# Opening loads of a fused attention and MLP kernel: another queue for the first v, w_in in more parts

## The chip, the cores and the metric

The kernel runs on one core of a Trainium2 chip. The metric is the device time of one execution in microseconds (us), lower is better. The time before is 259.38 us, the median of three runs (259.32 to 259.7).

## The reference

Eight batches of eight heads with 576 rows of 64 columns go through a linear attention: k and v are multiplied into a 64x64 matrix per head, q is multiplied by that, and each row is divided by its root mean square and scaled by g_norm. The result, 4608 rows of 512 columns, goes through a two-layer network with 2048 hidden columns and a sigmoid gate.

```
kv = np.einsum('bhsd,bhse->bhde', k, v)
out = np.einsum('bhsd,bhde->bhse', q, kv)
rms = np.sqrt(np.mean(out * out, axis=-1, keepdims=True) + 1e-06)
x = (out / rms * g_norm)          # then heads beside each other: 4608 x 512
h = x @ w_in                      # 512 x 2048
g = h * (1.0 / (1.0 + np.exp(-1.702 * h)))
return g @ w_out                  # 2048 x 512
```

Inputs and output are float32 in HBM; the kernel multiplies in float16.

## The kernel before

The rows are worked in nine tiles of 512 (`NT = B + 1`): tile t holds the first 512 rows of batch t, and tile 8 the remaining 64 rows of all batches. Tile t's two matrix products run while the attention of a later batch is put between them. Tiles 1 to 8 do both products by a scheme of seven products on halves (lines 589 and 709), with sums formed by VectorE. The order of work is written out by hand, engine by engine; each engine runs its own instructions in that order.

The change concerns the opening. The attention of batch 0 is computed in four head pairs (c = 0 to 3). For each pair TensorE transposes q (`a0.q(c)`, line 439, which needs the identity `ident`), multiplies k by v (`a0.kv(c)`, line 262), and VectorE masks the product with `ones2` (line 429). Then TensorE multiplies q by it (`a0.out(c)`, line 307), sums squares with `ones2` (`a0.ss(c)`, line 384), and VectorE scales (`a0.apply(c)`, line 394). Between these stand `busy` matmuls on zeros (line 869). Then the first layer of tile 0 follows (`Hidden.mm`, line 478), column block by column block of w_in in the order of `COLS`, and the second layer (`project_all`, line 822), in which four blocks of w_out's rows are used at a time. A block is 128 columns of w_in, or 128 rows of w_out; there are 16 of each.

Three queues start transfers. SyncE's queue loads pair 0's k, q and v as float32 into a staging tile `qf` (line 161), and ScalarE or VectorE casts them to float16 (lines 860 to 862). GpSimd's queue loads everything else and casts on the way: q, k, v of the pairs 1 to 3 (line 91), then w_in in parts (`load_w_in(f0, f1, k0, k1)`, line 180: column blocks f0 to f1, row blocks k0 to k1), then w_out (`load_w_out`, line 209) mixed with batch 1's q, k and v. Each load of GpSimd's queue waits until the eighth load before it has landed. ScalarE's queue loads g_norm.

The output of a tile is stored from `osb` by SyncE (line 852), the tiles in `HALVED` in two halves as soon as each half is complete, the others whole. There are two such buffers.

Of the kernel before, what the change touches and what calls it, by code (L numbers as in the profile page):

```python
# [8 lines left out]
F32 = mybir.dt.float32  # L9
# [3 lines left out]
P = 128  # L13
# [3 lines left out]
def kernel(  # L17
# [10 lines left out]
    nc = tc.nc  # L28

    B, H, S, D = q.shape  # L30
# [3 lines left out]
    FO = DFF // P  # L34
    KO = DM // P
# [7 lines left out]
    PE_ = 96  # L43
# [6 lines left out]
    stage = ctx.enter_context(tc.tile_pool(name="stage", bufs=4))  # L50
# [18 lines left out]
    vbuf = const.tile([P, NPAIR, 2 * NJ * D], F16)  # L69
    ident = const.tile([P, P], F16)  # L70
    ones2 = const.tile([P, P], F16)
# [15 lines left out]
    def early_src(n, b, c0, c1):  # L87
        return srcs[n][b, 2 * c0 : 2 * c1].rearrange("h (p j) d -> p h (j d)", j=NJ)

    def early_load(n, b, c0, c1):  # L90
        nc.gpsimd.dma_start(  # L91
            out=raw[n][0:PE_, c0:c1, :].rearrange("p c (l x) -> p (c l) x", l=2),
            in_=early_src(n, b, c0, c1),
        )
# [57 lines left out]
            )  # L152

    first = {}
    for n in "kqv":
        if n != "q":
            rows = stage.tile([P, 6, 2 * P], F32, name="qf", tag="qf", bufs=2)
            rows = rows.rearrange("p h x -> p (h x)")[0:PE_]
        first[n] = rows[:, (n == "q") * 2 * NJ * D :][:, 0 : 2 * NJ * D]
        dst, src = first[n].rearrange("p (h x) -> p h x", h=2), early_src(n, 0, 0, 1)  # L160
        nc.sync.dma_start(out=dst, in_=src)
    g_row = const.tile([1, D], F32)
    nc.scalar.dma_start(out=g_row, in_=g_norm.unsqueeze(0))
    nc.vector.memset(ident, 0.0)
    nc.vector.memset(kvb[1], 0.0)
    nc.gpsimd.affine_select(
        out=ident,
        in_=ident,
# [3 lines left out]
        pattern=[[-1, P]],  # L172
        channel_multiplier=1,
    )
    nc.gpsimd.memset(ones2, 0.0)
    nc.gpsimd.memset(ones2[0:D, 0:D], 1.0)
    nc.gpsimd.memset(ones2[D:P, D:P], 1.0)

    def load_w_in(f0, f1, k0=0, k1=KO):
        nc.gpsimd.dma_start(  # L180
            out=w_in_sb[:, k0:k1, f0 * P : f1 * P],
            in_=moe_w_in[k0 * P : k1 * P, f0 * P : f1 * P].rearrange(
                "(ko ki) f -> ki ko f", ki=P
            ),
        )

    for c in range(1, NPAIR):
        for n in "qkv":
            early_load(n, 0, c, c + 1)
# [4 lines left out]
    load_w_in(8, 10, 1, 3)  # L194
    load_w_in(0, 4, 3, KO)
    load_w_in(8, 10, 3, KO)
    load_w_in(10, 12)
    load_w_in(4, 6)
    load_w_in(6, 8)
    load_w_in(12, FO)  # L200

    nc.scalar.preload_act_table_set("abs_reciprocal_sqrt_and_small")
    nc.vector.memset(eps_t, EPS)
# [415 lines left out]
    class Seven:  # L619
# [60 lines left out]
        def place(self, name, mo, with_, i, j):  # L680
# [9 lines left out]
            if self.t == B:  # L690
# [3 lines left out]
                else:  # L694
                    store_rest(2 + mo, j * HN, (j + 1) * HN)
            elif self.t in HALVED and j == 1 - i:
                store(self.t, 2 * i, 2 * i + 2)
# [34 lines left out]
    def store_rest(mo, n0, n1):  # L732
        osb = osbs[B]
        for g in range(2):
            rows = out[(2 * mo + g) * S : (2 * mo + g + 1) * S, n0:n1]
            if 2 * mo + g < EARLY:
                p0 = SM % PE_
                rows = rows[bass.DynSlice(NJ * p0 + SM // PE_, R, step=NJ), :]
            else:
                rows = rows[SM:S, :]  # L740
            late = mo == 2 and n0 > 0
            queue = nc.gpsimd if mo == 0 or late else (nc.sync, nc.scalar)[g]
            queue.dma_start(out=rows, in_=osb[g * R : (g + 1) * R, mo, n0:n1])  # L743
# [43 lines left out]
    def layers(t, units1, units2):  # L787
# [11 lines left out]
        else:  # L799
            project_all(hid.gT, units2)  # L800
        if EARLY <= t < B and t not in HALVED:
            store(t, 0, J)
# [11 lines left out]
    def project_all(gT, units):  # L814

        os = {}

        def project(mo, fo):
            if fo == 0:
                pool, tag = (ps_h, "hT") if mo < 2 else (ps_o, "o")  # L820
                os[mo] = pool.tile([P, DM], F32, name="o", tag=tag)
            nc.tensor.matmul(  # L822
                os[mo],
                gT[:, fo, mo * P : (mo + 1) * P],
                w_out_sb[:, fo, :],
                start=(fo == 0),
                stop=(fo == FO - 1),
            )
            if fo == FO - 1:
                copy = nc.scalar.copy if mo % 2 else nc.vector.tensor_copy  # L830
                copy(osbs[0][:, mo, :], os[mo])

        steps = [(mo, 4 * i + k) for i in range(3) for mo in range(4) for k in range(4)]
        steps += [(mo, fo) for fo in (12, 13) for mo in range(4)]
        steps += [(mo, 14 + k) for mo in range(4) for k in range(2)]
        for n, (mo, fo) in enumerate(steps):
            project(mo, fo)
            for u in units.get(n, ()):
                u()
# [11 lines left out]
    def store(t, j0, j1):  # L851
        nc.sync.dma_start(
            out=out[t * S : t * S + SM, :].rearrange("(p j) m -> p j m", j=J)[:, j0:j1],
            in_=osbs[t][:, j0:j1],
        )
# [3 lines left out]

    nc.scalar.copy(qraw[0:PE_, 0, :], first["q"])  # L860
    nc.vector.tensor_copy(kraw[0:PE_, 0, :], first["k"])
    nc.vector.tensor_copy(vbuf[0:PE_, 0, :], first["v"])


    idle_ps = ps_h.tile([P, SM], F32, name="idle", tag="hT")
# [110 lines left out]
    def plan(t):  # L976
        return SECOND if t < EARLY else LATER if t < B - 1 else LAST_TWO

    HALVED = (2, 3, 4, 5)
    live = {0: a0}  # L980

    def start(b):
# [136 lines left out]
```

## Time and profile before

| what | value |
|---|---|
| median of three runs | 259.38 us |
| the profiled execution | 259.57 us |
| its span, first to last instruction | 257.8 us |
| TensorE (PE) busy | 249.9 us, 97% of the span |
| VectorE (DVE) busy | 193.8 us, 75% |
| ScalarE (ACT) busy | 177.0 us, 69% |
| GpSimd (POOL) busy | 59.6 us, 23% |
| granted TensorE clock | 0.999 |

Times in rows are us from the start of the span. In a row of a timeline stand the start, the duration, the engine, the line of the kernel, the operation and the tiles (written <- read), and in brackets how long the engine had been idle before and what ended that. PEld is TensorE's loading of weights, which runs beside its matmuls. A name followed by q (SPq, POOLq) is the queue that issues transfers. In rows of transfers stand the size of each as it is written, and the time from the start of the issue to the landing.

### The profile page before, as it was taken

The numbers are of one execution on the slowest core, as the hardware profiler recorded it, in microseconds if no ns is written. First come the engines' busy times: TensorE is split into PE (matmuls) and PEld (weight loads), VectorE is DVE, ScalarE is ACT, GpSimd is POOL, SyncE is SP. The second block draws the span as 40 slices with busy tenths as digits, with TensorE's granted clock in tenths as the row PEclk, the third lists the DMA queues.
The fourth block names the chain that finished last, engine by engine and source line by source line (L and its number), as shares of the span: only waits on it lengthen the run. The fifth ranks groups of instructions, "written<-read, shape, count | busy, mean of one in ns | idle before, by whom it ended". The sixth has DMA issues, their size and how long they took to land.

```text
span 257.8 us, 6355 instructions
## 1 busy us (share of the span) xinstructions
PE 249.9 (97%) x2596; PEld 203.6 (79%) x2596; DVE 193.8 (75%) x341; ACT 177.0 (69%) x322; POOL 59.6 (23%) x97
## 2 busy tenths in 40 slices
PE   7799999999999999999999999999999999999994
PEld 2443444788888888888888888898888888888883
DVE  1557565999958886798679867986899687857872
ACT  3468834988759894889579957995799469536800
POOL 8794245504071013301250134000000000000013
PEclk9999999999999999999999999999999999999999
DMA  7999999998999979999999799908600430012005
GB/s 175 195 168 203 204 203 200 191 160 134 194 157 200 153 90 189 184 290 112 188 184 162 84 204 144 183 4 130 210 4 0 84 163 3 0 60 106 3 19 145
DMA packets 69263, 35.33 MB, mean 137 GB/s; under 512 B 38034, under 2 KB 66834, under 8 KB 68978
## 3 DMA queue, kind: packets, MB, share of 16 engines
q0 software_dynamic: 38208, 18.31, 56.2%
q1 hardware_dynamic: 30624, 16.29, 27.2%
q8 instruction: 20, 0.33, 0.5%
q10 hardware_dynamic: 402, 0.33, 0.4%
q14 instruction: 9, 0.07, 0.1%
HBM read 36.70 MB, written 9.44 MB: 179 GB/s over the span
## 4 chain that ended last, share of the span: by engine, by line
PE 84%; DMA 11%; POOL 2%; issue 1%; DVE 0%
PE o L709 38%; PE h L589 38%; DMA w_out_sb<-in_moe_w_out_dram 7%; PE o L822 3%; DMA w_in_sb<-in_moe_w_in_dram 3%; DMA qraw<-in_q_dram 2%; POOL w_in_sb L180 2%; PE kvp L250 2%; PE outR L337 1%; PE ss L384 1%; PE kvp L262 0%; PE outT L307 0%; PE outT L311 0%; POOL vbuf L91 0%; DVE osb L689 0%
## 5 line engine op out<-in xcount | busy, mean ns | idle before, releaser
L566 ACT ACTIVATE gT<-h 128x512 f16<-128x512 f32 x96 | 52.4, 602 | 5.7 <-PE h L589 5.7
L589 PEld LDWEIGHTS <-ws 128*128 128x128 f16 x512 | 50.1, 98 | 5.9
L709 PEld LDWEIGHTS <-gS 128*128 128x128 f16 x512 | 49.1, 98 | 6.1 <-DVE gS L641 0.3
L589 PE MATMUL h<-xS,ws 128*128 128x256 f16 x384 | 52.2, 273 | 0.0
L709 PE MATMUL o<-tw,gS 128*128 128x256 f16 x384 | 45.6, 273 | 0.0
L589 PEld LDWEIGHTS <-w_in_sb 128*128 128x128 f16 x384 | 37.5, 98 | 4.7
L709 PEld LDWEIGHTS <-gT 128*128 128x128 f16 x384 | 37.6, 98 | 4.3
L709 PE MATMUL o<-w_out_sb,gT 128*128 128x256 f16 x256 | 31.4, 273 | 0.0
L589 PE MATMUL h<-xT,w_in_sb 128*128 128x256 f16 x224 | 31.1, 273 | 0.0
L603 DVE TENSOR_TENSOR h<-h,s 128x512 f32<-128x512 f32 x32 | 22.3, 698 | 4.6 <-PE h L589 3.0
L686 DVE TENSOR_TENSOR osb<-o,qf 128x512 f32<-128x512 f32 (+1 forms) x25 | 16.7, 668 | 11.3 <-PE o L709 11.3
L605 DVE TENSOR_TENSOR s<-h,s 128x512 f32<-128x512 f32 x32 | 22.1, 691 | 4.1 <-PE h L589 3.3
L743 POOL DMA_DIRECT2D out_dram<-osb x6 | 3.2, 539 | 93.2 <-DVE osb L686 93.2
L641 DVE TENSOR_TENSOR gS<-gT 128x512 f16<-128x512 f16 (+2 forms) x32 | 21.3, 684 | 0.7 <-ACT gT L566 0.6
L566 ACT ACTIVATE gT<-s 128x512 f16<-128x512 f32 x32 | 19.8, 628 | 2.8 <-DVE s L605 2.8
L589 PE MATMUL h<-xS,w_in_sb 128*128 128x256 f16 x128 | 18.9, 273 | 0.0
L535 DVE COPY s<-h 128x512 f32<-128x512 f32 x19 | 13.0, 685 | 7.7 <-PE h L589 7.6
L353 DVE TENSOR_REDUCE sum<-sq 128x8 f32<-128x512 f16 x24 | 14.9, 679 | 4.7 <-ACT sq L347 4.7
L325 ACT ACTIVATE sq<-outT 128x512 f16<-128x512 f32 (+1 forms) x16 | 7.8, 493 | 15.4 <-PE outT L307 9.9
L993 ACT ACT_TABLE_LOAD x14 | 18.0, 1283 | 0.2
L115 POOL DMA_DIRECT2D kraw<-in_k_dram x7 | 6.0, 856 | 48.6 <-PE kvp L250 32.7
L535 ACT COPY h<-h 128x512 f32<-128x512 f32 x27 | 15.4, 577 | 2.1 <-PE h L589 1.8
(105 smaller groups left out, 366.4 us busy)
## 6 DMA issues: line engine op xcount, KB each, us to landing
out_dram<-osb SPq DMA_DIRECT2D x8, 512.0 KB, 5.6
kraw<-in_k_dram POOLq DMA_DIRECT2D x5, 512.0 KB, 6.3
vbuf<-in_v_dram POOLq DMA_DIRECT2D x5, 512.0 KB, 9.8
out_dram<-osb SPq DMA_DIRECT2D x2, 1024.0 KB, 4.6
qraw<-in_q_dram POOLq DMA_DIRECT2D x3, 512.0 KB, 11.3
qbuf<-in_q_dram POOLq DMA_DIRECT2D x3, 512.0 KB, 12.5
out_dram<-osb SPq DMA_DIRECT2D x6, 192.0 KB, 6.5
w_out_sb<-in_moe_w_out_dram POOLq DMA_DIRECT2D x2, 512.0 KB, 12.7
```

The source lines that it names most:

```text
L325: nc.scalar.activation(sq[:, 0:n], t, AFT.Square)
L353: nc.vector.tensor_reduce(out=self.sum4[:, j, :], in_=self.o[j][1].rearrange("p (x d) -> p x d", d=D), op=ALU.add, axis=mybir.AxisListType.X,)
L535: (nc.vector.tensor_copy if engine == "D" else nc.scalar.copy)(to, src)
L566: nc.scalar.activation(self.gT[:, to, n * TH : (n + 1) * TH], src, AFT.Gelu_apprx_sigmoid)
L589: nc.tensor.matmul(bank[name][:, a], w, x, start=(p in (1, 5) and a == 0 and k == 0), stop=(k == KH - 1), skip_group_check=True,)
L603: nc.vector.tensor_add(bank["z"], bank["x"], self.s5)
L605: nc.vector.tensor_add(self.s5, bank["x"], self.s5)
L641: op(s[:, n, lo], a, b)
L686: nc.vector.tensor_add(o, ps, self.kept[with_][:, m])
L709: nc.tensor.matmul(o, a, w, start=(p in (1, 2, 5) and i == 0 and (mo == 0 or split)), stop=(i == HF - 1), skip_group_check=True,)
L822: nc.tensor.matmul(os[mo], gT[:, fo, mo * P : (mo + 1) * P], w_out_sb[:, fo, :], start=(fo == 0), stop=(fo == FO - 1),)
L993: u2.setdefault(i, []).append(lambda: f(*args))
```

## The change

Pair 0's v is no longer loaded by SyncE and cast by VectorE: it is GpSimd's first load, straight into `vbuf`. VectorE instead of GpSimd sets `ones2`, and GpSimd instead of VectorE clears `ident` before it writes the diagonal. The load of w_in's column blocks 10 and 11 is split by rows into two, that of blocks 12 to 15 by columns into two. Tile 6 joins the tiles that are stored in halves.

```
     first = {}
-    for n in "kqv":
-        if n != "q":
-            rows = stage.tile([P, 6, 2 * P], F32, name="qf", tag="qf", bufs=2)
-            rows = rows.rearrange("p h x -> p (h x)")[0:PE_]
+    rows = stage.tile([P, 6, 2 * P], F32, name="qf", tag="qf", bufs=2)
+    rows = rows.rearrange("p h x -> p (h x)")[0:PE_]
+    for n in "kq":
         first[n] = rows[:, (n == "q") * 2 * NJ * D :][:, 0 : 2 * NJ * D]
         dst, src = first[n].rearrange("p (h x) -> p h x", h=2), early_src(n, 0, 0, 1)
         nc.sync.dma_start(out=dst, in_=src)
...
-    nc.vector.memset(ident, 0.0)
     nc.vector.memset(kvb[1], 0.0)
+    nc.gpsimd.memset(ident, 0.0)
...
-    nc.gpsimd.memset(ones2, 0.0)
-    nc.gpsimd.memset(ones2[0:D, 0:D], 1.0)
-    nc.gpsimd.memset(ones2[D:P, D:P], 1.0)
+    nc.vector.memset(ones2, 0.0)
+    nc.vector.memset(ones2[0:D, 0:D], 1.0)
+    nc.vector.memset(ones2[D:P, D:P], 1.0)
...
+    early_load("v", 0, 0, 1)
     for c in range(1, NPAIR):
...
-    load_w_in(10, 12)
+    load_w_in(10, 12, 0, 2)
+    load_w_in(10, 12, 2, KO)
     load_w_in(4, 6)
     load_w_in(6, 8)
-    load_w_in(12, FO)
+    load_w_in(12, 14)
+    load_w_in(14, FO)
...
-    nc.vector.tensor_copy(vbuf[0:PE_, 0, :], first["v"])
...
-    HALVED = (2, 3, 4, 5)
+    HALVED = (2, 3, 4, 5, 6)
```

GpSimd's instructions at the start of the kernel, before (`qraw`, `kraw` and `vbuf` are the float16 tiles of q, k and v, `ones_98` is `ones2`; the loads of 96x2x384 are those of one head pair):

```order
L166 AFFINE_SELECT ident<-ident 128x128
L175 MEMSET ones_98 128x128
L176 MEMSET ones_98 64x64
L177 MEMSET ones_98 64x64
L91 DMA qraw<-in_q_dram 96x2x384
L91 DMA kraw<-in_k_dram 96x2x384
L91 DMA vbuf<-in_v_dram 96x2x384
```

The same place now, with the line numbers of the changed kernel:

```order
L164 MEMSET ident 128x128
L165 ISA
L165 AFFINE_SELECT ident<-ident 128x128
L91 DMA vbuf<-in_v_dram 96x2x384
L91 DMA qraw<-in_q_dram 96x2x384
L91 DMA kraw<-in_k_dram 96x2x384
L91 DMA vbuf<-in_v_dram 96x2x384
```

The memsets of the ones are gone, that of the identity is new, and one load stands ahead of the nine that were there.

Further on in GpSimd's order come the last loads of w_in and the first of w_out, before:

```order
L180 DMA w_in_sb<-in_moe_w_in_dram 128x256
L180 DMA w_in_sb<-in_moe_w_in_dram 128x4x256 x3
L180 DMA w_in_sb<-in_moe_w_in_dram 128x4x512
L209 DMA w_out_sb<-in_moe_w_out_dram 128x4x512
L91 DMA qraw<-in_q_dram 96x8x384
```

And now:

```order
L179 DMA w_in_sb<-in_moe_w_in_dram 128x256
L179 DMA w_in_sb<-in_moe_w_in_dram 128x2x256 x2
L179 DMA w_in_sb<-in_moe_w_in_dram 128x4x256 x4
L211 DMA w_out_sb<-in_moe_w_out_dram 128x4x512
L91 DMA qraw<-in_q_dram 96x8x384
```

Four loads have become six: two of two row blocks each for column blocks 10 and 11, then four of two column blocks each, where the last had four.

VectorE's first instructions, before (`kvb_88` is the tile on which the `busy` matmuls work, `qT` the transposed q, `kv_180` the product of k and v of pair 0):

```order
L164 MEMSET ident 128x64
L165 MEMSET kvb_88 128x256
L203 MEMSET eps_t 128x1
L205 MEMSET one_t 1x1
L861 COPY kraw<-qf 96x768
L862 COPY vbuf<-qf 96x768
L445 COPY qT<-q_163 128x576
L429 TENSOR_TENSOR kvb_87<-kv_180,ones_98 128x128
```

And now:

```order
L163 MEMSET kvb_88 128x256
L174 MEMSET ones_98 128x64
L175 MEMSET ones_98 64x64
L176 MEMSET ones_98 64x64
L205 MEMSET eps_t 128x1
L207 MEMSET one_t 1x1
L863 COPY kraw<-qf 96x768
L447 COPY qT<-q_163 128x576
L431 TENSOR_TENSOR kvb_87<-kv_180,ones_98 128x128
```

The cast of v between those of k and the copy of q is gone, and the three memsets of the ones stand ahead. TensorE's instructions and ScalarE's computing ones are in the same order as before.

## The prediction

> **What bounds the kernel now.** I read the page first, then the timeline of TensorE, the chain of waits, and the table by stage. The page says that TensorE is busy nearly always, apart from the opening, and that the transfers are busy all through the opening.
>
> ```profile
> span 257.8 us, 6355 instructions
> PE   7799999999999999999999999999999999999994
> DMA  7999999998999979999999799908600430012005
> ```
>
> The change touches the opening and one store near 205 us, so the question is what time the opening hands on to the rest. The table by stage (busy us of each engine with the number of its instructions, granted clock, DMA share, GB/s) has this for all that follows the opening:
>
> ```profile
> 47.00:257.80 210.80, 207.12 (x2262) 183.60 (x2260) 167.69 (x283) 150.78 (x281) 31.66 (x49) 1.00 0.76 125
> ```
>
> 207.1 of 210.8 us are TensorE's own work at full clock: whatever the opening is late or early at 47 us, the end is late or early by the same. In the opening, TensorE's timeline shows what it waits for:
>
> ```profile
> 13.34 0.38 PE L262 MATMUL kv<-vbuf,kraw 96*64 96x64 f16 x12 [0.62 <-DMA vbuf<-in_v_dram]
> 24.70 4.49 PE L478 MATMUL hT<-xT,w_in_sb 128*128 128x512 f16 x20 [0.55 <-DMA w_in_sb<-in_moe_w_in_dram]
> 34.27 3.40 PE L822 MATMUL o<-w_out_sb,gT 128*128 128x512 f16 x15
> 37.92 1.67 PE L822 MATMUL o<-w_out_sb,gT 128*128 128x512 f16 x7 [0.24 <-DMA w_out_sb<-in_moe_w_out_dram]
> ```
>
> The last wait is the one that counts. At 37.92 TensorE had been ready for 0.24 us and w_out's row blocks 10 and 11 were not there. Every microsecond that TensorE wins before 37.7 is lost there, unless that load comes earlier too. The chain of waits says how old that load is:
>
> ```profile
> 1.80 5.47 DMA qraw<-in_q_dram
> 21.11 16.76 DMA w_out_sb<-in_moe_w_out_dram
> 37.92 1.67 PE o L822 x7
> ```
>
> It is issued at 21.11 and lands 16.8 us later: it stands in a backlog. What moves it is not when GpSimd issues it but how fast the 16 DMA engines work off all that was queued ahead. That rate, by stage:
>
> ```profile
> 2.40:3.50 1.10, 1.10 (x4) 0.41 (x3) 0.00 (x0) 0.17 (x1) 1.10 (x3) 1.00 1.01 344
> 3.50:4.50 1.00, 1.00 (x4) 0.34 (x3) 0.46 (x1) 0.00 (x0) 1.00 (x2) 1.00 1.00 240
> 9.00:13.00 4.00, 3.19 (x65) 1.76 (x64) 2.31 (x6) 2.85 (x5) 3.11 (x6) 1.00 1.29 199
> 13.00:14.00 1.00, 0.66 (x14) 0.48 (x15) 1.00 (x3) 0.10 (x1) 0.80 (x2) 1.00 1.26 197
> 15.00:18.00 3.00, 3.00 (x15) 1.36 (x14) 1.87 (x4) 2.34 (x3) 3.00 (x4) 1.00 1.26 144
> 18.10:22.10 4.00, 4.00 (x24) 1.76 (x23) 1.66 (x3) 3.44 (x8) 2.78 (x4) 1.00 1.38 193
> 22.20:24.60 2.40, 1.96 (x10) 0.69 (x7) 2.33 (x5) 2.14 (x5) 0.69 (x1) 1.00 1.25 207
> 24.70:35.00 10.30, 10.29 (x68) 5.32 (x69) 6.54 (x16) 7.28 (x12) 3.07 (x5) 1.00 1.27 204
> ```
>
> The DMA share stays at 1.0 or above from 2.4 us on, so the engines are never short of work. Before 4.5 us the rate is that of SyncE's float32 loads; later it is that of GpSimd's loads, which are counted by the float16 that they write.
>
> **The change, part by part.** *Pair 0's v.* Now SyncE loads it as float32, VectorE casts it, and TensorE waits for the cast:
>
> ```profile
> 1.03 0.29 POOL L166 TENSOR_SCALAR_AFFINE_SELECT ident<-ident 128x128 f16<-128x128 f16 x1 [0.56 <-DVE ident L164]
> 1.26 0.20 POOL L175 MEMSET ones<- 128x128 f16 x1
> 1.80 0.79 POOL L91 DMA_DIRECT2D qraw<-in_q_dram  x1
> 6.84 0.11 PEld L262 LDWEIGHTS <-kraw 96*64 96x64 f16 x1 [0.42 <-issue]
> 7.03 0.60 DVE L862 CAST vbuf<-qf 96x768 f16<-96x768 f32 x1 [2.43 <-DMA qf<-in_v_dram]
> 7.67 0.38 PE L262 MATMUL kv<-vbuf,kraw 96*64 96x64 f16 x12 [0.77 <-DVE vbuf L862]
> qf<-in_v_dram SPq DMA_DIRECT2D x1, 288.0 KB, 5.3
> qraw<-in_q_dram POOLq DMA_DIRECT2D x1, 144.0 KB, 5.5
> ```
>
> GpSimd no longer waits 0.56 us for VectorE and does not set the ones (1.26 to 1.80); it gets the identity's memset instead (0.20, as the 128x128 one above). Its first issue moves from 1.80 to about 1.3. The first load of its queue took 5.5 us to land, so v would land at 6.8; with one SyncE load less beside it (288 KB is 295 kB, at 344 GB/s 0.86 us) at 5.9. Either way v is there when TensorE's weights for it are loaded (6.84), and kv starts near 6.9 instead of 7.67: 0.8 us won, and 0.60 us of VectorE with it. None of it lasts: at 13.34 TensorE waits for pair 3's v, which stands behind the same twelve loads as before. Counted: 0.
>
> *What v does to the backlog.* The same elements are read from HBM, by another queue. As SyncE's load it costs 295 kB / 344 = 0.86 us of all engines, as GpSimd's 147 kB / 199 = 0.74: -0.12 us. The bounds are the nearest rows on either side: if it was v's load that crawled at 240 GB/s from 3.5 to 4.5, its 1.23 us go and the gain is -0.49; if it runs at 144 GB/s as the loads at 15 to 18 do, it takes 1.02 and costs +0.16. I take -0.12, since 9 to 13 us holds just such q, k and v loads.
>
> *w_in's column blocks 12 to 15 in two parts.* GpSimd issues blocks 10-11, 4-5, 6-7 and 12-15 in a row from 13.49 to 16.47; the first lands 6.0 us after its issue, at 19.5, the last 9.0 after its own (the last 0.77 us of the four), at 24.7:
>
> ```profile
> 13.49 2.98 POOL L180 DMA_DIRECT2D w_in_sb<-in_moe_w_in_dram  x4 [0.20 <-issue]
> w_in_sb<-in_moe_w_in_dram POOLq DMA_DIRECT2D x1, 256.0 KB, 6.0
> w_in_sb<-in_moe_w_in_dram POOLq DMA_DIRECT2D x1, 512.0 KB, 9.0
> ```
>
> So 22.2 to 24.6 is the load of blocks 12-15, in rows of 512 columns, at 207 GB/s, and 18.1 to 22.1 are the three loads in rows of 256 columns, at 193. In two parts blocks 12-15 come in rows of 256 columns too. Their 512 KB (524 kB) take 2.53 us at 207 and 2.72 at 193: +0.19 us for everything behind, w_out's rows among it. Bounds: 0, if the slower stretch owes its rate to its place and not to its rows, and 524 / 144 = 3.64, so +1.11, if the parts run like the small ones at 15 to 18. Nothing in the rows points below zero. I take +0.19, from the loads of the same shape. What TensorE gets for it is the 0.55 us wait at 24.70: blocks 12 and 13 land some 1.3 us before 14 and 15, so it goes. But TensorE then only stands 0.24 + 0.55 = 0.8 us before 37.92.
>
> *Blocks 10 and 11 in two parts, and three more issues.* The rows keep their length here. TensorE's third matmul on block 10 now waits for the second part, which ends where the whole load ended. That two more transfers cost next to nothing show the first three parts of w_in, 128 KB each (the first and the third issue, and their times to landing):
>
> ```profile
> 8.33 0.56 POOL L180 DMA_DIRECT2D w_in_sb<-in_moe_w_in_dram  x1
> 9.86 0.53 POOL L180 DMA_DIRECT2D w_in_sb<-in_moe_w_in_dram  x1 [0.21 <-issue]
> w_in_sb<-in_moe_w_in_dram POOLq DMA_DIRECT2D x1, 128.0 KB, 5.5
> w_in_sb<-in_moe_w_in_dram POOLq DMA_DIRECT2D x1, 128.0 KB, 5.3
> ```
>
> They land at 13.8 and 15.2, so 0.7 us apart, which is the time of 131 kB at 197 GB/s, the rate from 13 to 14; just before it was 199. That is 0.01 us each, +0.02 for two. Each issue takes GpSimd 0.5 to 0.8 us and waits until the eighth transfer before it has landed; with 16.8 us between issue and landing neither makes w_out late.
>
> [...]
>
> *Ones by VectorE, identity by GpSimd.* Three small memsets on VectorE before 1.5 us; its first cast waits for k until 4.04. 0.
>
> ```profile
> 4.04 0.56 DVE L861 CAST kraw<-qf 96x768 f16<-96x768 f32 x1 [2.81 <-DMA qf<-in_k_dram]
> ```
>
> *Tile 6 in halves.* The whole store is issued behind the last copy of its tile:
>
> ```profile
> 203.28 0.69 DVE L686 TENSOR_TENSOR osb<-o,qf 128x512 f32<-128x512 f32 x1 [0.65 <-PE o L709]
> 205.02 0.59 ACT L689 COPY osb<-o 128x512 f32<-128x512 f32 x1 [2.26 <-PE o L709]
> 205.63 0.33 SPq L852 DMA_DIRECT2D out_dram<-osb  x1
> 248.91 0.69 DVE L686 TENSOR_TENSOR osb<-o,qf 128x512 f32<-128x512 f32 x1 [0.62 <-PE o L709]
> ```
>
> The first half can go at 204.0, the second at 205.6. The next writer of that buffer is tile 8's, at 248.9, and nothing else on SyncE's queue stands behind it then. 0; it costs one issue of 0.33 us on an idle queue.
>
> **Sum.** -0.12 + 0.19 + 0.02 = +0.09 us at w_out's row blocks 10 and 11, handed on whole. The profiled execution took 259.57 us (span 257.8), the median is 259.38: 259.66 on the first, 259.47 on the second. With both bounds taken together the backlog moves between -0.5 and +1.3.
>
> **Rivals.** *The whole queue moves with its start.* The chain begins at GpSimd's first issue. If the backlog keeps its distance to that, w_out comes up to 0.5 us earlier, and v's crawl at 240 GB/s goes with it. For it: the slow row at 3.5 to 4.5, before GpSimd's data flow. Against it: a DMA share of 1.0 there, so an earlier issue finds engines that have work. Price: -0.5 for the start, -0.12 for v, nothing for the parts: -0.6, so 258.8. TensorE can follow, as it is ready 0.8 us earlier. It decides if that load lands before 37.4.
>
> *The smaller parts slow the queue.* The new parts stand just behind the stretch at 144 GB/s, where four small parts of w_in run, three of them in rows of 256 columns. If that rate is theirs and the new parts prolong it, blocks 12 to 15 cost up to +1.11: half to all of it gives 259.9 to 260.5, say 260.3. For it: 144 against 199 with the DMA share still at 1.26, so the time goes into the transfers. Against it: three 256-column loads right behind run at 193. It decides if the load lands after 38.4.
>
> *Each added part pays its way alone.* If a part had to be confirmed before the next one's data could flow, it would cost what an early load takes beyond its data:
>
> ```profile
> qf<-in_k_dram SPq DMA_DIRECT2D x1, 288.0 KB, 3.3
> ```
>
> That is 3.3 - 0.86 = 2.4 us, twice 4.9: 264.3. The three parts that land 0.7 us apart speak against it: 1 in 100. [...]
>
> *v comes late through GpSimd's queue,* after 7.7, so that the change doesn't do what it says: the 0.62 us wait at 13.34 covers it, and the time is the forecast's.
>
> **How the numbers follow.** The forecast, with v late or not: 0.55, 259.1 to 259.8. The whole queue earlier: 0.24. Smaller parts slow: 0.20. Parts that pay alone: 0.01. 0.2% is 0.52 us, about what a measurement of this kernel can tell from no change. So faster 0.24, same 0.55, slower 0.21. The predicted time is the forecast's on the median, 259.4 in round figures. The range 258.7 to 260.2 takes in the forecast's, most of the earlier queue and the milder half of the slow parts.
>
> **What would show it.** Right: kv of pair 0 starts near 6.9, the wait for pair 3's v at 13.34 grows, the wait at 24.7 is gone or below 0.1 us, and TensorE resumes on w_out's row blocks 10 and 11 between 37.5 and 38.4 after a wait of some 0.8 us. Wrong: no wait there at all (then TensorE, not the backlog, was the bound), a landing outside those ends, or a difference in span that arises after 47 us, where I count nothing.

## The result, and the profile after

The changed kernel takes 260.48 us (median of 11 executions, 259.56 to 261.44), the kernel before beside it 259.14 us (11 executions, 258.29 to 260.09). The ratio is 1.0049, with a 95% interval of 1.0033 to 1.0065: some 1.3 us slower. The forecast was no change, 259.4 us; the measured time lies outside its range.

The profiled execution of the changed kernel took 260.42 us. Its page begins almost as the one before did, with a span 0.9 us longer:

```profile
span 258.7 us, 6355 instructions
PE   8789999999999999999999999999999999999994
DMA  7999999999999969999999699908600620012005
```

TensorE's timeline in the opening, the rows that answer to those shown of before (lines are shifted by two):

```profile
6.67 0.60 PE L870 MATMUL idle<-kvb 128*128 128x512 f16 x2
7.21 0.38 PE L264 MATMUL kv<-vbuf,kraw 96*64 96x64 f16 x12
9.37 0.38 PE L264 MATMUL kv<-vbuf,kraw 96*64 96x64 f16 x12 [0.45 <-DMA vbuf<-in_v_dram]
11.70 0.38 PE L264 MATMUL kv<-vbuf,kraw 96*64 96x64 f16 x12 [0.80 <-DMA vbuf<-in_v_dram]
13.91 0.38 PE L264 MATMUL kv<-vbuf,kraw 96*64 96x64 f16 x12 [0.69 <-DMA vbuf<-in_v_dram]
21.98 7.24 PE L480 MATMUL hT<-xT,w_in_sb 128*128 128x512 f16 x32
38.91 1.67 PE L824 MATMUL o<-w_out_sb,gT 128*128 128x512 f16 x7 [0.45 <-DMA w_out_sb<-in_moe_w_out_dram]
```

Pair 0 starts earlier, at 7.21 instead of 7.67, and the wait for w_in at 24.70 is gone: 32 matmuls run through from 21.98. But pair 3's v, which let TensorE go on at 13.34, does so at 13.91, and w_out's row blocks 10 and 11 at 38.91 instead of 37.92. Pair 1 now waits as well, and pair 2 for 0.80 us instead of 0.27. GpSimd's first issue is 0.27 us earlier than the 1.80 of before, and carries v:

```profile
1.53 0.79 POOL L91 DMA_DIRECT2D vbuf<-in_v_dram  x1 [0.22 <-issue]
```

The chain of waits runs through pair 2's v, which lands at 11.56, then parts of w_in, and ends at the same load of w_out:

```profile
5.42 6.14 DMA vbuf<-in_v_dram
23.65 15.21 DMA w_out_sb<-in_moe_w_out_dram
38.91 1.67 PE o L824 x7
```

Behind the opening, the stage in which the prediction counted no difference has none. The row of the table by stage differs from that of before by 0.3 us in its length and by as much in TensorE's work:

```profile
48.17:258.70 210.53, 206.81 (x2261) 183.16 (x2259) 167.51 (x283) 150.50 (x281) 31.60 (x49) 1.00 0.76 125
```

Where the opening lost is seen in the transfers. First the changed kernel by stage (the last three columns: granted clock, DMA share, GB/s), then two stretches of the kernel before that were not shown yet:

```profile
2.40:3.50 1.10, 1.10 (x4) 0.45 (x3) 0.00 (x0) 0.17 (x1) 1.10 (x2) 1.00 0.94 334
3.50:4.50 1.00, 1.00 (x4) 0.30 (x2) 0.70 (x1) 0.00 (x0) 1.00 (x3) 1.00 1.11 212
4.00:7.00 3.00, 3.00 (x20) 1.03 (x18) 0.82 (x2) 0.83 (x1) 3.00 (x6) 1.00 1.08 144
9.00:13.00 4.00, 2.71 (x50) 1.51 (x52) 2.06 (x5) 1.92 (x4) 3.12 (x6) 1.00 1.29 196
18.00:22.00 4.00, 4.00 (x24) 1.87 (x23) 2.04 (x3) 3.18 (x7) 3.49 (x5) 1.00 1.27 151
```

```profile
4.00:7.00 3.00, 2.70 (x21) 0.99 (x19) 0.56 (x1) 0.83 (x1) 3.00 (x5) 1.00 1.14 211
18.00:22.00 4.00, 4.00 (x23) 1.79 (x22) 1.66 (x3) 3.35 (x7) 2.84 (x4) 1.00 1.39 193
```

From 4 to 7 us, where SyncE's v had been moving, 144 GB/s flow instead of 211, with the DMA share at 1.08 instead of 1.14 (v counts 288 KB as SyncE's load and 144 KB as GpSimd's). From 9 to 13 the rates are the same (196 and 199). A second stretch, 18 to 22, is slower too (151 against 193).

This one profile ran at full clock. Not all single executions did: of the 11, seven had a mean granted clock of 0.984 to 0.993 over the span, and their median is 260.63; the median of the four at 1.0 is 259.97. So some 0.8 us of the loss are there at full clock too.

### The profile page after: what moved, and what is told of

Its sections match the earlier page's. It is cut to its first block, busy times and chain, and to the rows that moved or that the text cites. A ratio compares the mean times of both kernels' runs of the same rounds, so it can differ in the third digit from the quotient of the medians.

```text
span 258.7 us, 6355 instructions
## 1 busy us (share of the span) xinstructions
PE 250.9 (97%) x2596; PEld 203.5 (79%) x2596; DVE 194.2 (75%) x342; ACT 176.9 (68%) x322; POOL 61.5 (24%) x98
## 4 chain that ended last, share of the span: by engine, by line
PE 84%; DMA 11%; POOL 3%; issue 1%; DVE 0%; POOLq 0%
PE o L711 38%; PE h L591 38%; DMA w_out_sb<-in_moe_w_out_dram 6%; DMA w_in_sb<-in_moe_w_in_dram 3%; PE o L824 3%; DMA vbuf<-in_v_dram 2%; PE kvp L252 2%; POOL w_in_sb L179 2%; PE outR L339 1%; PE ss L386 1%; POOL vbuf L91 1%; POOL qraw L91 0%; POOL kraw L91 0%; PE kvp L264 0%; PE outT L309 0%
## 5 line engine op out<-in xcount | busy, mean ns | idle before, releaser
L591 PEld LDWEIGHTS <-w_in_sb 128*128 128x128 f16 x384 | 37.4, 98 | 4.8
L711 PEld LDWEIGHTS <-gT 128*128 128x128 f16 x384 | 37.5, 98 | 4.4
L388 ACT ACTIVATE rs<-ss,eps_t 128x512 f32<-128x512 f32 (+1 forms) x16 | 9.2, 580 | 11.8 <-PE ss L386 11.8
```

The costliest lines, as they stand in the source:

```text
L388: nc.scalar.activation(rs[:, 0:n], t[:, 0:n], AFT.Abs_reciprocal_sqrt, bias=eps_t, scale=1.0 / D)
L591: nc.tensor.matmul(bank[name][:, a], w, x, start=(p in (1, 5) and a == 0 and k == 0), stop=(k == KH - 1), skip_group_check=True,)
L711: nc.tensor.matmul(o, a, w, start=(p in (1, 2, 5) and i == 0 and (mo == 0 or split)), stop=(i == HF - 1), skip_group_check=True,)
```

## The experiments

The texts on record speak of four theories. A: GpSimd's queue delays itself, because it now issues its loads without a pause. B: the added parts of w_in are slow. C: TensorE idles more in the opening, and its clock is then lowered. D: SyncE's v cost GpSimd's queue nearly nothing, so its removal frees nothing. Beside each ratio to the kernel before stands how many executions had a mean clock under 0.995. Of the 138 executions of the kernel before that were timed beside the experiments, 20 had.

### The parts of the change

**v first, with the memsets.** e1 is the change without the four parts of w_in and without tile 6:

```
-    load_w_in(10, 12, 0, 2)
-    load_w_in(10, 12, 2, KO)
+    load_w_in(10, 12)
...
-    load_w_in(12, 14)
-    load_w_in(14, FO)
+    load_w_in(12, FO)
...
-    HALVED = (2, 3, 4, 5, 6)
+    HALVED = (2, 3, 4, 5)
```

> The kernel before with pair 0's v as GpSimd's first load, VectorE setting the ones and GpSimd the identity; w_in's loads and tile 6's store as before. Theory A (GpSimd writing descriptors without a pause slows the transfers of its queue about a microsecond later): GpSimd issues nine loads without a pause from 1.5 to 7.3 us, the rate from 5.5 to 8 us falls below that of before, pair 3's v lands near 13.8 instead of 13.2, and all behind it by as much: w_out's blocks 10 and 11 near 38.4, +0.2%. Theory B (the added parts of w_in are slow by themselves, v is not to blame): landings as before or earlier, w_out near 37.8, no change. My prediction's own sum for this part: -0.12 us.

Measured: 260.97 us, 1.0064 (1.0041 to 1.0087); 8 of 12 under 0.995. These two pieces alone do at least what the whole change does. The way is not that of theory A: in e1's profile w_out's blocks 10 and 11 land at 37.4 us, not at 38.4, and TensorE does not wait for them.

**Four parts.** e2 is the kernel before with only those two splits:

> The kernel before with w_in's blocks 10-11 and 12-15 in two parts each, all else as before. Theory A: GpSimd now issues without a pause for 1.4 us longer, so the stretch of slow transfers that ended near 18 us before lasts to 20 us or beyond, in the loads of blocks 4-5 and 6-7 too, whose shape is the same as before; w_out's blocks 10 and 11 land 0.4 to 0.8 us later, TensorE resumes near 38.5. Theory B: the loads of blocks 4-7 run at 193 GB/s as before and only the new parts are slow; w_out 0.2 to 1.1 later. My prediction's sum for this part: +0.21 us.

Measured: 259.45 us, 1.0011 (0.9989 to 1.0033); none of 12. No cost that this measurement can tell from nothing.

**Memsets and tile 6.** e3 is the kernel before with VectorE's and GpSimd's memsets swapped and tile 6 in halves, f3 the swap alone:

```
-    nc.vector.memset(ident, 0.0)
     nc.vector.memset(kvb[1], 0.0)
+    nc.gpsimd.memset(ident, 0.0)
...
-    nc.gpsimd.memset(ones2, 0.0)
+    nc.vector.memset(ones2, 0.0)
...
-    HALVED = (2, 3, 4, 5)
+    HALVED = (2, 3, 4, 5, 6)     # e3 only
```

> The kernel before with VectorE setting the ones, GpSimd the identity, and tile 6 stored in halves; v and w_in's loads as before. All theories: GpSimd's first issue moves from 1.8 to about 1.5 us, nothing else; the time within 0.1% of before. If the whole backlog moved with GpSimd's first issue, it would be 0.3 us less.

> Of the change only the swap of the memsets (VectorE the ones, GpSimd the identity), v still SyncE's. With tile 6 in halves the two together gave 1.0024. Theory A: GpSimd's first load is issued some 0.3 us earlier, but the loads land no earlier: 1.001 to 1.003, nearly all of the pair's 1.0024. If tile 6's halves cost it instead, this run gives 0.999 to 1.001. Theory C: one run in six or fewer at a clock under 0.995.

Measured: e3 259.48 us, 1.0024 (1.0007 to 1.0041), 2 of 12; f3 259.62 us, 1.0020 (1.0001 to 1.0039), 2 of 12. Tile 6 costs nothing that shows. The swap seems to cost 0.2%, and its own profile does not show where: the span is that of before, 257.8 us.

**Pauses for GpSimd.** e4 is the changed kernel with a memset of 128x256 on GpSimd ahead of each of the last six loads of w_in (six lines of this kind):

```
+    nc.gpsimd.memset(gap_t, 0.0)
     load_w_in(10, 12, 0, 2)
```

> The changed kernel with a memset of 128x256 on GpSimd (about 0.35 us, on a tile that nobody reads) ahead of each of the last six loads of w_in, so that GpSimd does not write descriptors without a pause there; the loads themselves are the same. Theory A: from 18 to 22 us the transfers run above 180 GB/s instead of about 150, and w_out's blocks 10 and 11 land 0.4 to 0.8 us earlier than in the changed kernel, near 38.2; time 0.15 to 0.3% less than the changed kernel's. Theory B: the rate from 18 to 22 stays about 150, and the time is that of the changed kernel.

Measured: 260.76 us, 1.0066 (1.0045 to 1.0087); 3 of 6. Pauses bring nothing: from 18 to 22 us 164 GB/s flow, where theory A had asked for more than 180, and w_out's blocks land at 38.5, not near 38.2. Theory A loses its support there.

**All but v.** h1 is the changed kernel with v as SyncE's third load again:

```
-    early_load("v", 0, 0, 1)
...
+    nc.vector.tensor_copy(vbuf[0:PE_, 0, :], first["v"])
```

> The changed kernel with pair 0's v as SyncE's third load again: the swapped memsets, the four parts of w_in and tile 6 in halves stay. If v's move is what harms (its 0.6 us of GpSimd's queue, and the clock), what is left is the memsets' 0.2% and the parts' 0.1% at most: 1.001 to 1.003, at most two runs in twelve under a clock of 0.995. If the parts cost the 0.4 us by which w_out's blocks 10 to 11 land later still after the opening, it is 1.003 to 1.005 without any early v.

Measured: 259.80 us, 1.0019 (1.0004 to 1.0034); 1 of 12. That is what the swap alone measures. With v on SyncE's queue the parts add nothing, as in e2, and the larger part of the loss goes with v. Theory B, by which the parts are to blame by themselves, falls. What they do beside an early v is another question, taken up below.

**v alone.** f2 is the kernel before with only v moved:

```
-    for n in "kqv":
+    for n in "kq":
...
+    early_load("v", 0, 0, 1)
     for c in range(1, NPAIR):
...
-    nc.vector.tensor_copy(vbuf[0:PE_, 0, :], first["v"])
```

> Of the change only v's move to GpSimd's queue; the memsets as before, no added parts, tile 6 as before. If v's move alone is what harms, the ratio is 1.004 to 1.008, as with v and the memsets together (1.0064), with part of the runs at a clock under 0.995. If it takes the swapped memsets too (GpSimd issues without a pause from 1.5 us), v alone gives 0.999 to 1.002 and clocks of 0.997 or more.

Measured: 260.80 us, 1.0064 (1.0043 to 1.0085); 6 of 9. Its timeline for pair 3's v:

```profile
14.06 0.53 PE L262 MATMUL kv<-vbuf,kraw 96*64 96x64 f16 x12 [0.68 <-DMA vbuf<-in_v_dram]
```

14.06 against 13.34: with one load more in GpSimd's queue pair 3 is 0.72 us late, nearly a whole load (0.74 us by the prediction's rates). These are two single profiles, and profiles scatter, so here are all of them (landings in us, issue and time to landing taken together):

| pair 0's v | w_in's parts | profiles | pair 3's v lands | w_out's blocks 10 and 11 land |
|---|---|---|---|---|
| SyncE | as before | before, e3, f3, f4, g4 | 12.8 to 13.8 | 36.3 to 38.1 |
| SyncE | four parts | e2, h1 | 13.0, 13.5 | 37.6, 37.7 |
| GpSimd | as before | e1, f2, g3, k1 | 13.5 to 14.0 | 37.4 to 38.6 |
| GpSimd | four parts | the changed kernel, e4, f1 | 13.3 to 13.9 | 38.5 to 38.9 |
| left out | as before | g1 | 13.1 | 37.4 |
| ScalarE | as before; h3 the last one split | g2, h2, h3 | 12.6 to 12.7 | 36.4 to 36.5 |

The mean landing of pair 3's v is 13.21 in the seven with v on SyncE's queue and 13.76 in the seven with it on GpSimd's: 0.5 us for one load more. For w_out's blocks 10 and 11 the table says something that the times of e1, e2 and h1 do not: in all three profiles that have both the early v and the parts these blocks land late, and TensorE waits for them. h1, g3 and f1, in this order:

```profile
34.71 4.91 PE L824 MATMUL o<-w_out_sb,gT 128*128 128x512 f16 x22
34.65 4.91 PE L822 MATMUL o<-w_out_sb,gT 128*128 128x512 f16 x22
38.77 1.67 PE L824 MATMUL o<-w_out_sb,gT 128*128 128x512 f16 x7 [0.18 <-DMA w_out_sb<-in_moe_w_out_dram]
```

In the first two, 22 matmuls run through without a wait. With one profile for each kernel this is a pattern and no proof: f2, without the parts, comes to 38.6 as well, though TensorE is not held up there, and before and f3 have a wait of 0.24 and 0.30 us with a landing near 37.8. Why v and the parts together should be late is not shown.

### What SyncE's v had cost

g1 is the kernel before without that load. Pair 0's v is left out of the computation, and k stands in its place:

```
-    for n in "kqv":
+    for n in "kq":
...
-    nc.vector.tensor_copy(vbuf[0:PE_, 0, :], first["v"])
+    nc.vector.tensor_copy(vbuf[0:PE_, 0, :], first["k"])
```

> The kernel before without SyncE's load of pair 0's v at all (pair 0 takes k's values in its place; nothing is added to GpSimd's queue). It measures what that load costs GpSimd's queue. The prediction's step gave it 295 kB/344 = 0.86 us of all engines: then the first of GpSimd's loads (q of pair 1, landed at 7.27 us before) and pair 3's v (13.20 before) land 0.7 to 0.9 us earlier, at about 12.4, and the time falls by 0.3 to 0.8 us. Theory D: SyncE's v rides in engine time that GpSimd's queue cannot use in its first microseconds, so taking it away moves pair 3's v by 0.3 us at most and the ratio stays at 0.999 to 1.001; the load it becomes in GpSimd's queue then costs its whole 0.74 us, less the 0.27 us of the earlier issue.

Measured: 259.79 us, 1.0021 (1.0002 to 1.0039); 7 of 12. Its rows by stage and on TensorE's timeline:

```profile
4.00:7.00 3.00, 3.00 (x19) 1.10 (x16) 0.94 (x2) 0.83 (x1) 3.00 (x5) 1.00 1.08 146
```

```profile
13.19 0.38 PE L262 MATMUL kv<-vbuf,kraw 96*64 96x64 f16 x12 [0.63 <-DMA vbuf<-in_v_dram]
```

Less work does not make this kernel faster. The ratio lies above both ranges that had been expected, but seven executions lost clock; the median of the five others is 259.26, that of the kernel before at full clock. Pair 3's v comes 0.15 us earlier, which is within the scatter above, where 0.86 us of engine time had been counted as freed. From 4 to 7 us only 146 GB/s flow, as in the changed kernel (144), against 211 in the kernel before: with SyncE's load gone, GpSimd's queue does not take up the engines' time that this load had used. This is what theory D says.

### The clock

e1's profile is one of the executions at a lower clock. Its table by stage (granted clock third from the end):

```profile
10.00:14.00 4.00, 2.13 (x51) 1.32 (x50) 2.33 (x5) 1.54 (x3) 3.02 (x6) 1.00 1.28 197
13.00:14.00 1.00, 0.36 (x15) 0.32 (x13) 0.92 (x2) 0.42 (x1) 0.71 (x2) 1.00 1.25 201
14.00:15.00 1.00, 1.00 (x6) 0.36 (x4) 0.39 (x2) 0.48 (x1) 1.00 (x2) 0.57 1.31 189
15.00:16.00 1.00, 1.00 (x4) 0.32 (x3) 0.75 (x1) 0.40 (x2) 1.00 (x2) 0.50 1.31 186
16.00:17.00 1.00, 1.00 (x4) 0.44 (x3) 0.00 (x0) 0.40 (x1) 0.80 (x2) 0.50 1.31 155
17.00:18.00 1.00, 1.00 (x5) 0.35 (x3) 0.00 (x0) 0.17 (x1) 0.47 (x1) 0.72 1.33 174
18.00:19.00 1.00, 1.00 (x7) 0.47 (x5) 0.45 (x1) 0.98 (x2) 1.00 (x2) 1.00 1.43 182
```

TensorE is busy 2.13 of the 4 us from 10 to 14, and then its clock is halved: (0.43 + 0.50 + 0.50 + 0.28) / 0.50 = 3.4 us at half. Over a span of 259 us, 3.4 us at half make a mean of 0.993, and 6.8 us one of 0.987. Of the 39 executions under 0.995 of the kernels with an early v and no filling (the changed one, e1, e4, f2) and of g1 and f4, 30 have just these means. (A mean of 0.997 to 0.999 need not come from the opening: in the profile of before, with 0.999, the clock is 1.00 in every stretch up to 257 us and 0.68 from there to 257.8, where TensorE, last busy at 254.1, has no work left.) The same 4 us in the profile of before, and in that of the changed kernel, which kept its clock:

```profile
10.00:14.00 4.00, 2.97 (x54) 1.69 (x54) 2.74 (x7) 2.35 (x4) 3.23 (x6) 1.00 1.28 200
```

```profile
10.00:14.00 4.00, 2.39 (x45) 1.33 (x46) 2.22 (x6) 2.35 (x4) 2.90 (x6) 1.00 1.28 199
```

Within a kernel, the executions at a lower clock are the longer ones in e1 (median 261.36 against 259.29 at full clock) and in the kernel before (259.96 against 259.07 beside f1), but not in f2 (260.77 against 260.88 in three) and e4 (260.64 against 260.88, three each). So the clock is put to the test by itself.

**Less work for TensorE.** f4 is the kernel before without the four idle matmuls behind pair 0's q and kv:

```
     a0.q(0)
-    busy(2)
     a0.kv(0)
...
-    busy(2)
     a0.out(0)
```

> The kernel before without the four idle matmuls behind pair 0's q and kv (two and two, 0.22 us each warm); nothing else. Theory C: TensorE idles 0.87 us more between 6 and 14 us, so part of the runs, a third or more, should show a clock under 0.995 and a time 1 to 2 us longer; the ratio 1.002 to 1.006. Theory A: no load lands later and pair 3's v still sets the end of the stage, so the ratio is 0.999 to 1.001.

Measured: 260.03 us, 1.0025 (1.0003 to 1.0046); 8 of 12. In its profile the clock is at half for two such stretches, from between 10 and 11 us to just behind 17:

```profile
10.00:11.00 1.00, 0.96 (x18) 0.74 (x20) 0.00 (x0) 0.99 (x2) 0.53 (x1) 0.67 1.32 201
11.00:12.00 1.00, 1.00 (x16) 0.49 (x13) 0.91 (x3) 0.18 (x1) 0.92 (x2) 0.50 1.30 200
17.00:18.00 1.00, 1.00 (x6) 0.43 (x5) 0.00 (x0) 0.55 (x1) 1.00 (x2) 0.91 1.40 184
```

From 7 to 11 us, towards the end of which it falls, TensorE is busy for 3.02 of 4 us, more than in the stretch of the changed kernel that kept its clock:

```profile
7.00:11.00 4.00, 3.02 (x66) 1.95 (x64) 1.93 (x6) 1.59 (x3) 2.79 (x5) 0.92 1.30 195
```

So the busy share of TensorE alone does not decide; what else does is not shown. No load was touched. Four matmuls on zeros less are enough to bring the lower clock from 20 in 138 to 8 in 12, and 0.25%.

**The waits filled.** f1 is the changed kernel, g3 is e1, g4 the kernel before, and k1 is f2, each with idle matmuls where TensorE waits for v. In f1, g3 and k1:

```
     a0.q(1)
+    busy(2)
     a0.kv(1)
...
     a0.q(2)
+    busy(3)
     a0.kv(2)
...
     a0.q(3)
+    busy(2)
     a0.apply(1)
```

g4 has only the last two, with 1 and 2.

> The changed kernel with 2, 3 and 2 more idle matmuls (0.22 us each) behind the query transposes of pairs 1, 2 and 3, where TensorE waits 0.45, 0.80 and 0.69 us for pair v's landing. Theory C (the clock): the early v makes TensorE idle more between 9 and 14 us, and in part of the executions the granted clock then falls to half for one or two stretches of about 3.4 us from 14 us on (a mean clock of 0.993 or 0.987 where the kernel before has 0.997 to 1.0). With the waits filled every run should have a clock of 0.997 or more, and the ratio to the kernel before should fall from 1.005 to 1.001-1.003. Theory A (GpSimd's queue is slowed by its own dense issues): the landings are untouched, so the ratio stays at 1.004 to 1.007 whatever TensorE does in between.

> v first on GpSimd with the swapped memsets (1.0064 without more, 8 of 12 runs at a clock under 0.995), and the waits for pairs 1 to 3's v filled with 2, 3 and 2 idle matmuls; no added parts, tile 6 as before. Theory C: no run under 0.997, and the ratio falls to what its runs at full clock had, 1.001 to 1.002. Without the clock as a cause it stays at 1.005 to 1.008.

> The kernel before with 1 and 2 idle matmuls ahead of pair 2's and pair 3's kv, where TensorE waits 0.27 and 0.62 us. Theory C: 8 of the 61 runs of the kernel before were at a clock of 0.993 and some 0.8 us longer, and with the waits filled none is, so the ratio is 0.999 to 1.000. Against it: the filling only delays TensorE, 1.001 to 1.003.

> Only v's move to GpSimd's queue (1.0064 alone, 6 of 9 runs at a clock under 0.995), with 2, 3 and 2 idle matmuls in the waits for pairs 1 to 3's v; memsets, w_in and tile 6 as before. Theory C with theory D: every run at a clock of 0.997 or more, and what is left is the queue's own delay of 0.6 to 0.7 us at pair 3's v, of which the backlog hands on most: 1.001 to 1.003. If the clock is all of it, 0.999 to 1.001. If it is none of it, 1.005 to 1.008.

| kernel | filled | not filled |
|---|---|---|
| the changed kernel (f1) | 1.0031 (1.0008 to 1.0054), none of 12 | 1.0049 (1.0033 to 1.0065), 7 of 11 |
| v first, with the memsets (g3) | 1.0019 (1.0002 to 1.0037), none of 12 | 1.0064 (1.0041 to 1.0087), 8 of 12 |
| v alone (k1) | 1.0041 (1.0026 to 1.0056), none of 8 | 1.0064 (1.0043 to 1.0085), 6 of 9 |
| the kernel before (g4) | 0.9996 (0.9979 to 1.0013), none of 12 | 1, 20 of 138 |

In none of these 44 executions with filled waits is the mean clock under 0.995; the lowest is 0.997. TensorE does more work, and the three kernels with an early v measure 0.2 to 0.45% less. For v with the memsets the two intervals lie apart; in the other two pairs they overlap. Theory C holds, and in g3 it is all that can be told, for the 0.19% left there is what the swap alone measures. It is not the whole everywhere: with the clock held, v alone still costs 0.41%. k1's profile shows how its delay is handed on to the wait that stood at 24.70 before:

```profile
25.63 4.49 PE L478 MATMUL hT<-xT,w_in_sb 128*128 128x512 f16 x20 [0.61 <-DMA w_in_sb<-in_moe_w_in_dram]
```

That is 0.93 us late. As k1 then waits for no block of w_out, the last row of this product in TensorE's timeline starts at 46.89 instead of 46.36: 0.53 us of the delay are left in this profile, half of the 0.41% (1.06 us) that the medians give.

### The opposite: v on a queue that starts early

If engine time before 7 us is there for the queues of SyncE and ScalarE but not for GpSimd's, v should go to the earliest of these. g2 is the kernel before with v on ScalarE's queue, h2 adds one idle matmul each ahead of pair 2's and pair 3's kv, h3 adds to h2 the split of w_in's column blocks 12 to 15:

```
-        nc.sync.dma_start(out=dst, in_=src)
+        (nc.scalar if n == "v" else nc.sync).dma_start(out=dst, in_=src)
...
     a0.q(2)
+    busy(1)                      # h2, h3
...
     a0.q(3)
+    busy(1)                      # h2, h3
...
-    load_w_in(12, FO)
+    load_w_in(12, 14)            # h3
+    load_w_in(14, FO)
```

> The kernel before with pair 0's v issued on ScalarE's queue, ahead of the row of the norm, in place of third on SyncE's; nothing else. If the opening has engine time to spare before GpSimd's first packet at 4.2 us, v lands beside k and q, by 5.5 to 6 us in place of 7.0, GpSimd's loads meet fewer rivals after that, pair 3's v lands 0.2 to 0.4 us earlier, and the ratio is 0.998 to 1.000. If the three loads only share the same engine time, v lands at 6.5 to 7, k and q later, and the ratio is 1.000 to 1.002.

> The kernel before with pair 0's v on ScalarE's queue (0.9992 alone, pair 3's v landed at 12.62 us) and one idle matmul each ahead of pair 2's and pair 3's kv. Theory C: no run under a clock of 0.995. The queue starts on GpSimd's loads sooner: ratio 0.997 to 0.999. If the idle matmuls only delay TensorE, 1.000 to 1.001.

> The same with w_in's columns 12 to 15 in two parts, so that the wait of 0.4 to 0.6 us for them at 24.5 us goes. If that wait is worth something, 0.996 to 0.999; if the bound is still the landing of w_out's blocks 10 to 11, the same as without the parts to 0.001; if added parts cost the queue something, 1.000 to 1.002.

Measured: g2 258.95 us, 0.9992 (0.9977 to 1.0008), 1 of 12; h2 259.01 us, 0.9987 (0.9968 to 1.0006), none of 12; h3 258.58 us, 0.9974 (0.9961 to 0.9988), none of 12. h3 is faster than both kernels; g2 and h2 cannot be told from the kernel before. Its profile, by stage, then on ScalarE's queue, then on TensorE:

```profile
3.50:4.50 1.00, 1.00 (x4) 0.35 (x3) 0.00 (x0) 0.00 (x0) 1.00 (x3) 1.00 1.09 340
4.00:7.00 3.00, 2.59 (x7) 0.61 (x4) 1.30 (x2) 0.83 (x1) 3.00 (x6) 1.00 1.21 226
```

```profile
0.76 0.44 ACTq L161 DMA_DIRECT2D qf<-in_v_dram  x1
```

```profile
13.22 0.38 PE L263 MATMUL kv<-vbuf,kraw 96*64 96x64 f16 x12
33.57 4.91 PE L823 MATMUL o<-w_out_sb,gT 128*128 128x512 f16 x22
```

v is issued at 0.76 instead of 1.70 us, the rate from 3.5 to 4.5 is 340 GB/s instead of 240, pair 3's v lands at 12.6, earlier than in any profile with v on another queue, and w_out's blocks 10 and 11 at 36.4. Neither is waited for any more: 22 matmuls on w_out run through, as in most of the profiles above, where before there were 15, a wait, and 7. h2's profile has the same two TensorE rows at the same times, so what the split in h3 adds is not shown.

## Why the prediction was wrong

**The step that failed is v's move to the backlog, counted at -0.12 us.** It took 0.86 us off the engines for SyncE's load and put 0.74 on for GpSimd's. The second term was near: one load more makes pair 3's v 0.5 us late in the mean of seven profiles, 0.72 in f2. The first was not there: without SyncE's load, pair 3 gains 0.15 us (g1), not 0.86. At the landing for which the sum was made, w_out's blocks 10 and 11, +0.09 was counted and +0.99 came, 38.87 instead of 37.88; with everything but v it is 37.7 (h1). With the clock held, v's move alone costs 1.06 us of the time (k1). What misled was the sentence that a DMA share of 1.0 or more means engines that are never short of work. From 4 to 7 us the changed kernel moves 144 GB/s at a share of 1.08 and from 9 to 13 us 196 at 1.29; the kernel before moved 144 at 1.26 from 15 to 18 us. In these rows the share says that transfers are open, not that the engines move all they can. The bounds of the term, -0.49 to +0.16, came from rates of single rows and left out the case in which the load had been free.

The price of v's move is not one constant that can be added to others, either. In the changed kernel the first issue comes 0.27 us earlier, at 1.53 instead of 1.80 (about 1.3 was counted); g3, which has v and the earlier issue, measures 0.19% where k1, with v alone, has 0.41%, and w_out's blocks land late in all three profiles of v beside the parts, but only in one of four (f2) without them. Why is open.

**What had no step at all is the clock.** The stage table of before shows 1.00 in every row, and waits ahead of pair 3's v were priced at nothing because that v covers them. They have a price. The wait at 11.70 and its neighbours bring TensorE to 2.4 busy us of 4, and in 7 of 11 executions the mean clock is below 0.995. In the changed kernel filling the waits takes the ratio from 1.0049 to 1.0031, about 0.5 us, with intervals that overlap; in e1 it takes 1.0064 to 1.0019, with intervals that don't. In e1's profile the granted clock stands at 0.50 for 3.4 us, in f4's for 6.8, twice as long. It fell at the end of stretches in which TensorE was busy for 2.13 of 4 us (e1) and 3.02 of 4 (f4), and did not fall after 2.39 of 4 in the profile of the changed kernel. What sets the moment and the length of the fall is not shown.

**What was right.** Pair 0's kv starts earlier and nothing of it lasts. It came at 7.21, not near 6.9: its weights were waiting for no load, and the idle matmuls ahead of it, from 6.67 on, ended only then. The wait at 24.70 is gone. The splits alone cost nothing that can be told from nothing: +0.21 us was counted, and h1 with them measures what f3 does without them; the rival of parts that pay alone, at 4.9 us, falls with it. Tile 6's halves cost nothing that shows. No difference arises behind 47 us.

**What the text had named as wrong** happened: a landing outside 37.5 to 38.4. TensorE resumed at 38.91, after 0.45 us where some 0.8 were forecast. By its own sign, a landing after 38.4, this is the rival of the smaller parts, and its 259.9 to 260.5 holds the measured 260.48. Its cause is borne out by half. The stretch behind the new parts of blocks 10 and 11 is slower: from 18 to 22 us 149 to 164 GB/s flow in the five profiles that have them, 184 to 201 in the 13 that don't. But e2 and h1 have these parts without the early v, and w_out's blocks land there at 37.6 and 37.7, no later than before. One of the five is h1:

```profile
18.00:22.00 4.00, 4.00 (x24) 1.85 (x22) 1.64 (x4) 3.18 (x8) 3.34 (x6) 1.00 1.20 149
```

What the parts cost beside an early v is not shown by the times: with the clock held it is 0.31% with them (f1) and 0.19% without (g3), and the intervals overlap.

The rival of an earlier queue saw that v's crawl at 240 GB/s from 3.5 to 4.5 mattered, but read it the wrong way round: with one SyncE load less that stretch runs at 212 GB/s, with v beside it on ScalarE's queue at 340.

**The memsets,** counted at 0, measure 0.20% (f3), and 0.19% in h1. Both intervals barely leave out zero. With v first the same swap seems to go with a gain (g3 against k1), and nothing in f3's profile explains the loss: this stays open.

**The sum, then:** 0.19% with everything but v (h1), 0.12% more with v while the clock is held (f1), 0.18% more when it is not, 0.49% in all. The intervals are about 0.2% wide on each side, so this is a division of the measured loss and not three measured terms. A slip of the text changes nothing in this: its sum on the median, 259.47, is 259.5 in round figures and not 259.4.

## What to carry to other kernels

Before a load is moved to another queue, ask in which microseconds each queue can use the engines at all: a load on a queue that starts early may be free (pair 3's v came only 0.15 us earlier without SyncE's load, g1), and the same load can cost most of its time at the head of the queue on which the rest of the opening hangs (0.5 of the 0.74 us counted, in the mean of seven profiles). A DMA share near 1 does not answer that (144 GB/s at 1.08, 196 at 1.29); the GB/s of the stretch, and a kernel without the load, do. And a wait that "costs nothing" on TensorE can cost its clock (8 of 12 executions under 0.995 in e1, none of 12 with the waits filled in g3): look at the granted clock of single executions, and where it falls in an opening with little work, try idle matmuls in the waits. And one profile of each kernel is little: pair 3's v landed between 12.8 and 13.8 us in seven profiles that had the same loads ahead of it.

## What the runs showed of the hardware that was not expected

- The granted TensorE clock fell to 0.50 for 3.4 us (e1) or for 6.8, two such stretches (f4), in the midst of work, at the end of 4 us in which TensorE was busy for 2.13 (e1) and for 3.02 (f4), but not after 2.39 of 4 in the profile of the changed kernel. So the busy share alone does not tell when it falls. Of the changed kernel, e1, e4, f2, g1 and f4, 39 of 62 executions had a mean under 0.995; of the kernels with filled waits (f1, g3, g4, k1, h2, h3) none of 68.
- Taking a load of 288 KB out of the opening left pair 3's v on the other queue nearly where it was (13.19 instead of 13.34 us, g1). Without it only 146 GB/s flowed from 4 to 7 us at a DMA share of 1.08, against 196 to 199 at 1.29 from 9 us on. What limits GpSimd's queue at its start the rows do not show.
